# Soft-capped attention with a soft mixture of experts: ten instead of twelve output tiles stored by halves

## The chip, the core and the metric

The kernel runs on one core of a Trainium2 chip. The metric is the time of one execution on the device in microseconds (us). The core has five engines that run side by side and wait for each other by semaphores: PE multiplies matrices, DVE and ACT work element by element and are the ones that empty PE's accumulators (PSUM), POOL does the rest of the elementwise work and issues loads, and SP only issues transfers. The transfers themselves are carried by 16 DMA engines that all queues share.

## The reference

Two layers follow each other. The first is attention with a soft cap, for 8 batches, 12 heads, 448 tokens and 64 columns a head:

```
scores = cap * tanh(scale * q @ k.T / cap)
attn   = softmax(scores)
x      = (attn @ v), heads side by side: 3584 tokens x 768 columns
```

The second is a soft mixture of 8 experts with 4 slots each. Softmax over the tokens sends them into 32 slots, each expert runs two weight matrices over its slots, and softmax over the slots mixes the results back:

```
logits     = x @ phi                          # 3584 x 32
slot_input = softmax(logits, over tokens).T @ x
slot_out   = relu(slot_input @ w1[e]) @ w2[e] # 32 x 768
out        = softmax(logits, over slots) @ slot_out   # 3584 x 768, float32
```

What matters here is the last line: an output of 3584 x 768 floats, 11.01 MB, which must be written to DRAM, and which can be written only once slot_out is known.

## The kernel before, in words

**The long part.** The first 240 us or so are attention, with the logits and slot sums of the second layer woven in by a schedule written out by hand. Their order isn't touched by the change.

**The second layer's weights.** `layer1` (the first weight matrix, L1018) and `layer2` (the second, L1046) follow. The second matrix lies partly in SBUF (`w2b`) and partly in a DRAM copy that SP reads back (`w2t`, L997). `layer2` runs over 64 blocks twice, once for each half of the 768 output columns: the loop at L1099 makes `so[0]` (columns 0 to 383 of slot_out), the loop at L1106 makes `so[1]` (columns 384 to 767). `so[0]` is copied out of PSUM by ACT at L1104, `so[1]` by DVE at L1113.

**The output tiles.** The 3584 tokens are 28 tiles of 128 tokens. Tile n belongs to pair of batches `bb` = n // 7 and has place `c` = n % 7 in it; partition p of it holds token 896 bb + 7 p + c. So tiles that follow each other in one pair of batches hold neighbouring rows of the output, and two of them stored together are 6144 contiguous bytes a partition. Each tile is a matrix product of `et_tile` (the transposed exponentials) with `so`, then a multiplication by `winv` (one over the softmax sum) on the way from PSUM to SBUF, then a store by SP.

A tile goes out in one of two ways, and the constants `NH` and `NHL` (L1097) say which:

- Tiles 0 to NH - 1 go by halves, with `half_tile` (L1080). The first half (columns 0 to 383, called F here, so F10 is that of tile 10) needs only `so[0]`. F0 to F(NHL - 1) are made within the loop of `layer2` over the second half (L1109 to L1112), two a step on ACT and DVE and then one a step on ACT. F(NHL) to F(NH - 1) are made after it (L1114), with ACT for even tiles and DVE for odd ones; PE runs their products while DVE copies `so[1]`. Every F is a store of its own, 192 KB in rows of 1536 bytes. The second half (S) of the tiles below NH is made at L1130, with DVE for even tiles and ACT for odd ones. Two neighbouring S are stored together (384 KB, rows of 1536 bytes), unless the tile is the last of its pair of batches or the last below NH (L1092).
- Tiles from NH on go whole (W): two products into one PSUM tile (L1133), one multiplication over all 768 columns (ACT for even tiles at L1142, DVE for odd ones at L1140), and two neighbours stored together, 768 KB in rows of 6144 bytes (L1145). The seventh tile of a pair of batches is stored alone, as 384 KB.

**What else hangs on NH.** The transposition of the last two batches' exponentials (`e_transp`, L692 and L696) and their sums (`e_sums`, L705 and L706) stand in the same loop ahead of tiles NH + 3, NH + 5 and NH + 7. The PSUM tiles `op` of that loop come from a pool of three (L1128), so that the product of tile n waits until tile n - 3 has left PSUM. They take the place of the banks used before (`bank`, L1110 and L1115), so the first three of them wait for whoever read those banks last. The SBUF tiles `obh` (halves) and `ob` (whole) rotate through the eight places of tag `w1`; a place that held a stored tile is free when its store has landed.

**Order.** Each engine works through its instructions in the order of the program. SP issues the stores in the order F, S, W, and each store waits for the engines that wrote its source.

Of the kernel before, what the change touches and what calls it, by code (L numbers as in the profile page):

```python
# [37 lines left out]
def kernel(  # L38
# [1055 lines left out]
            return  # L1094
        store(k, half, half + 1, obs[bb, half][:, c - (n - k):c + 1, :], n - k + 1)

    NH, NHL = 12, 10  # L1097
    n2 = len(blocks)
    for n0 in range(0, n2, 4):  # L1099
        if n0 == n2 // 2 - 16:  # L1100
# [81 lines left out]
```

## Time and profile before

| what | value |
|---|---|
| median of 3 runs (lowest to highest) | 288.38 us (287.92 to 288.79) |
| the profiled execution, its own time | 288.24 us |
| its span, first to last instruction | 286.5 us |
| ACT, PE, DVE, POOL busy over the span | 89%, 87%, 85%, 48% |
| last product of PE ends | about 274 us |
| last store is issued | 276.0 us |
| stores of halves / of whole tiles | 19 / 9 |

The profiled execution is one of the program on the chip. Times within it are us from the first instruction. Shares of busy time are averages over the span; the part that the change touches is the last 31 us, from 255.6 us, when the first store is issued. GB/s are the bytes that the core's DMA engines moved in a stretch, and "DMA share" is how busy the 16 of them were (it can pass 1, since a DMA engine can have two packets under way).

### The profile page before, as it was taken

To read this page: it belongs to the slowest core of one execution; us is meant where nothing else is said; L and a number is where in the kernel's file an instruction comes from. 1 tells how busy PE (TensorE), PEld (TensorE's weight loads), DVE (VectorE), ACT (ScalarE), POOL (GpSimd) and SP (SyncE) were. 2 spreads that over 40 slices of the span, in tenths; PEclk is the share of its full clock that TensorE was granted. 3 is DMA by queue.
4 is the path that set the end of the run, shared out by engine and by line. 5 is a ranking of instruction groups with operands and counts; after the bars stand their busy time and mean duration, and the time that the engine had idled before them with its cause. 6 is when DMAs were issued, how large, how long until landed. Compare 5 with 4: busy or idle time off the path is not lost.

```text
span 286.5 us, 10763 instructions
## 1 busy us (share of the span) xinstructions
PE 250.3 (87%) x4706; PEld 170.3 (59%) x4706; DVE 242.6 (85%) x502; ACT 254.6 (89%) x211; POOL 138.9 (48%) x197
## 2 busy tenths in 40 slices
PE   8888889998999899989998999899899999998710
PEld 7555466756675666566656675667565767642400
DVE  3498999999999999999999999999999986437830
ACT  4999999999999999999999999999999997247720
POOL 7982655664765566555756646574563120200000
PEclk9999999999999999999999999999999999999975
DMA  7999999999999999999999999999999567989995
GB/s 241 257 205 205 201 194 204 224 205 206 232 230 196 209 232 225 217 206 231 227 216 198 226 224 211 214 226 222 206 182 226 137 247 223 409 326 392 414 420 244
DMA packets 58334, 68.11 MB, mean 238 GB/s; under 512 B 4144, under 2 KB 54448, under 8 KB 58288
## 3 DMA queue, kind: packets, MB, share of 16 engines
q0 software_dynamic: 42448, 35.31, 79.1%
q1 hardware_dynamic: 15552, 31.89, 31.7%
q8 instruction: 37, 0.61, 0.8%
q10 hardware_dynamic: 288, 0.23, 0.2%
q14 instruction: 9, 0.07, 0.1%
HBM read 91.72 MB, written 19.27 MB: 387 GB/s over the span
## 4 chain that ended last, share of the span: by engine, by line
DVE 40%; PE 33%; issue 10%; ACT 8%; POOL 5%; DMA 1%; DVEq 0%; ACTq 0%; SPq 0%
PE pv L590 9%; DVE xq L600 7%; PE sc L320 5%; DVE xp L570 4%; DVE xT L652 4%; DVE ex L571 4%; ACT ex L329 4%; DVE xp L568 3%; ACT ex L334 3%; DVE qT L279 3%; POOL vbd L287 2%; DVE ex L564 2%; DVE xp L569 2%; PE so_ps L1046 2%; DVE xf L566 2%
## 5 line engine op out<-in xcount | busy, mean ns | idle before, releaser
L329 ACT ACTIVATE ex<-sc 128x1344 f16<-128x1344 f32 (+1 forms) x113 | 148.3, 1428 | 1.4 <-PE sc L320 1.4
L334 ACT ACTIVATE ex<-ex 128x2688 bf16<-128x2688 f16 (+5 forms) x58 | 115.1, 1993 | 0.1
L590 PE MATMUL pv<-vbd,ex 128*128 128x130 bf16 (+1 forms) x1610 | 95.0, 211 | 11.4 <-POOL vbd L287 8.5
L590 PEld LDWEIGHTS <-ex 128*128 128x128 bf16 (+1 forms) x1680 | 75.7, 101 | 35.9 <-PE sc L320 9.0
L320 PE MATMUL sc<-qT,kT 64*64 64x448 bf16 x672 | 71.4, 360 | 0.5 <-DVE qT L279 0.4
L287 POOL CAST vbd<-vraw 64x896 bf16<-64x896 f32 x46 | 45.9, 998 | 49.5 <-issue 24.5
L600 DVE TENSOR_TENSOR xq<-pv,rec 128x448 bf16<-128x448 f32 x46 | 28.7, 625 | 1.6
L320 PEld LDWEIGHTS <-kT 64*64 64x64 bf16 x672 | 24.1, 105 | 6.3 <-issue 4.0
L295 POOL MEMSET vbd<- 64x1 bf16 x22 | 3.6, 165 | 45.7 <-PE pv L590 45.7
L570 DVE TENSOR_TENSOR xp<-xp,xf 128x1344 f16<-128x1344 f16 (+2 forms) x34 | 25.1, 738 | 0.8
L568 DVE TENSOR_TENSOR xp<-xp,xf 128x1344 f16<-128x1344 f16 (+2 forms) x34 | 25.0, 736 | 0.6
L116 POOL DMA_DIRECT2D w1b<-in_moe_w_dram x32 | 25.3, 792 | 0.0
L571 DVE TENSOR_TENSOR ex<-ex,xp 128x1344 uint16<-128x1344 uint16 (+2 forms) x34 | 24.7, 727 | 0.4
L567 DVE TENSOR_SCALAR xp<-xf 128x1344 f16<-128x1344 uint16 (+2 forms) x34 | 16.8, 494 | 0.4
L184 POOL DMA_DIRECT2D qb<-in_q_dram x22 | 16.7, 757 | 0.5 <-DMA kraw<-in_k_dram 0.5
L279 DVE COPY kT<-kps 128x896 bf16<-128x896 bf16 x23 | 14.2, 617 | 3.0 <-PE kps L274 2.8
L572 DVE TENSOR_SCALAR ex<-ex 128x1344 uint16<-128x1344 uint16 (+2 forms) x34 | 16.5, 485 | 0.1
L277 PEld LDWEIGHTS <-qb 128*64 128x64 bf16 x308 | 10.1, 109 | 10.9 <-issue 10.9
L184 POOL DMA_DIRECT2D kb<-in_k_dram x22 | 16.2, 735 | 0.1
L569 DVE TENSOR_SCALAR xp<-xp 128x1344 f16<-128x1344 f16 (+2 forms) x34 | 15.7, 462 | 0.6
L120 POOL DMA_DIRECT2D w2d<-in_moe_w_dram x21 | 15.9, 777 | 0.4 <-issue 0.4
L620 PE MATMUL pv<-ones 128*128 128x57 bf16 x376 | 16.0, 188 | 0.0
(124 smaller groups left out, 342.1 us busy)
## 6 DMA issues: line engine op xcount, KB each, us to landing
w1b<-in_moe_w_dram POOLq DMA_DIRECT2D x32, 384.0 KB, 9.1
vraw<-in_v_dram SPq DMA_DIRECT2D x44, 224.0 KB, 6.0
w2d<-in_moe_w_dram POOLq DMA_DIRECT2D x21, 384.0 KB, 8.1
w2t<-w2d SPq DMA_DIRECT2D x21, 384.0 KB, 7.1
out_dram<-ob SPq DMA_DIRECT2D x7, 768.0 KB, 8.2
qb<-in_q_dram POOLq DMA_DIRECT2D x22, 224.0 KB, 7.6
kb<-in_k_dram POOLq DMA_DIRECT2D x22, 224.0 KB, 6.1
w2b<-in_moe_w_dram POOLq DMA_DIRECT2D x11, 384.0 KB, 8.1
```

What stands on the lines that cost most here:

```text
L116: pool.dma_start(out=w1b[e][:, js, fs], in_=w1r[:, e, js, fs])
L184: pool.dma_start(out=t, in_=quad_ap(nm, Q))
L279: dve.tensor_copy(t, ps)
L287: pool.tensor_copy(vbds[Q % 2][r, :, :, c0:c0 + DH], raw[r])
L320: pe.matmul(sc[cs, u, 0:S], qkT["k", Q][r, c, cs], qkT["q", Q][r, :, cs], start=True, stop=True)
L329: act.activation(exs[j][:, half * CS + u0:half * CS + u1, :].bitcast(F16), (own[0] if i == u0 == 0 else sc)[:, u0:u1, 0:S], ACT.Tanh, scal ...
L334: act.activation(exs[j][:, u0:u1, :], exs[j][:, u0:u1, :].bitcast(F16), ACT.Exp, scale=cap)
L568: lambda: dve.tensor_tensor(p, p, f, op=ALU.mult),
L570: lambda: dve.tensor_tensor(p, p, f, op=ALU.mult),
L571: lambda: dve.tensor_tensor(y, y, p, op=ALU.add),
L590: pe.matmul(out_, exs[j][r, u, q0:q0 + (HP if tail else P)], v_, start=(c == 0 and g == gs[0] < NF), stop=(c == NT - 1), skip_group_check= ...
L600: dve.tensor_tensor(xq[Q][:, h, s0:s1, :], pv[:, 0:s1 - s0, 0:DH], rec.to_broadcast([P, s1 - s0, DH]), op=ALU.mult)
```

## The change

One constant goes from 12 to 10:

```diff
-    NH, NHL = 12, 10
+    NH, NHL = 10, 10
```

With it the loop at L1114 is empty, so F10 and F11 fall away, with their two products on PE, one multiplication each on ACT and DVE, and two stores. S0 to S9 are made as before, but S9 is now the last below NH and stored alone; S10 (which was stored with S9) and S11 (stored alone) fall away, again with one multiplication each on DVE and ACT. Tiles 10 and 11 become whole tiles: four products, one multiplication of 768 columns on ACT and one on DVE, and one store of 768 KB. The transpositions and sums of the last two batches now stand ahead of tiles 13, 15 and 17 instead of 15, 17 and 19. In counts: 28 stores become 26 (16 of halves, 10 of whole tiles); PE has the same products in another order; ACT and DVE have one instruction fewer each. The bytes written stay the same. POOL's instructions, and those of all engines ahead of L1113, are the same.

## The prediction

> **What bounds the kernel now.** I read the end of the execution first, since every edit lies there. The stretches of busy time:
>
> ```profile
> core 0: us, PE busy (x) PEld busy (x) DVE busy (x) ACT busy (x) POOL busy (x), PEclk, DMA share, GB/s
> ...
> 257.00:261.50 4.50, 4.06 (x42) 1.18 (x35) 3.00 (x6) 3.26 (x6) 0.00 (x0) 1.00 1.05 392
> ...
> 264.00:268.00 4.00, 3.46 (x23) 1.89 (x22) 3.40 (x6) 3.42 (x5) 0.00 (x0) 1.00 1.07 398
> 269.00:272.00 3.00, 1.98 (x11) 1.00 (x11) 2.46 (x3) 1.96 (x3) 0.00 (x0) 1.00 1.02 425
> 276.00:283.00 7.00, 0.00 (x0) 0.00 (x0) 0.00 (x0) 0.00 (x0) 0.00 (x0) 0.50 1.02 424
> ```
>
> The last two columns carry it. The DMA share is 1.02 to 1.07 from 257 us on, and after 276 us no engine computes: the transfers alone set the end, at 392 to 398 GB/s while rows of 1536 bytes go out (halves) and 424 or 425 with rows of 6144 (whole tiles). A DMA engine that never rests turns every pause in its supply into a later end. So the question isn't what ACT or DVE save but whether the stores still arrive without a gap. The transfers from 255 us on:
>
> ```profile
> issues: line engine op xcount, KB each, median us to landing
> out_dram<-ob SPq DMA_DIRECT2D x7, 768.0 KB, 8.2
> out_dram<-obh SPq DMA_DIRECT2D x14, 192.0 KB, 2.5
> out_dram<-obh SPq DMA_DIRECT2D x5, 384.0 KB, 3.7
> ```
>
> A small store lands 2.5 us after its issue, a whole pair 8.2 us: early stores hardly queue, late ones stand behind a long queue. So the early part is where a missing store can be felt. The chain of waits says what comes at the change:
>
> ```profile
> 259.68 0.57 DVE so L1113
> 260.25 0.04 issue
> 260.29 0.35 PE op L1086
> 260.64 0.03 issue
> 260.68 0.62 DVE obh L1088
> ```
>
> The S products need `so[1]`, whose copy ends at 260.25. F10 and F11 aren't on this chain. The timeline beside it:
>
> ```profile
> 259.22 1.29 ACT L1090 ACTIVATE obh<-op,winv 128x384 f32<-128x384 f32 x2
> ...
> 259.56 0.50 PE L1086 MATMUL op<-so,ET 128*128 128x384 bf16 x2
> 259.68 0.56 DVE L1113 CAST so<-so_ps 128x384 bf16<-128x384 f32 x1 [1.25 <-PE so_ps L1046]
> 260.15 2.38 DVE L1088 TENSOR_SCALAR obh<-op,winv 128x384 f32<-128x384 f32 x4
> ...
> 260.92 0.58 ACT L1090 ACTIVATE obh<-op,winv 128x384 f32<-128x384 f32 x1 [0.41 <-PE op L1086]
> ```
>
> The two products at 259.56 are F10 and F11; they run during the copy. ACT's group from 259.22 is F9 and F10, DVE's from 260.15 starts with F11, and 260.92 is S1 on ACT.
>
> **What is removed: supply.** Issue times on SP, from the trace: F0 255.64, then one F each 0.43 to 0.51 us up to F9 260.05, F10 260.56, F11 261.05; S0+S1 261.56, S2+S3 262.31, S4+S5 262.83, S6 263.34, S7+S8 264.03, S9+S10 264.94, S11 265.48, W12+W13 266.42.
>
> Each F is 196,608 bytes, 0.50 us at 392 GB/s; they come every 0.50 us, so supply and DMA go in step. In the trace's single packets (128 an F, counted in order) F0's first starts 0.84 us after its issue, with nothing ahead of it but 25 to 49 GB/s of leftover reading, and each from F2 to F11 1.00 us after. So only 0.16 us of work waits ahead of any F. F9's last packet starts at 261.56, F10's and F11's fill 261.56 to 262.58, and S0+S1 follows at 262.58. Without F10 and F11 the DMA engines have nothing after 261.56 until S0+S1 has been issued and has waited its 0.84 us.
>
> When is S0+S1 issued? Before, S1 leaves ACT at 261.50 and SP issues at 261.56, 0.06 later. S1's product started at 260.56, 0.05 after ACT had finished F10 (259.93 + 0.58 = 260.51): its PSUM bank was held by F10. In the new order of instructions that wait for ACT is gone, and S1's product can follow S0's (260.29) at PE's step between products of one tile, 0.16 us (264.36 to 264.52). So S1's product starts at 260.45, 0.11 earlier; ACT begins at 260.81 and ends at 261.39; SP issues at 261.45; first packet 261.45 + 0.84 = 262.29. **The gap is 262.29 - 261.56 = 0.73 us.**
>
> Bounds. If S1 isn't earlier and its first packet takes the loaded 1.02 us of the trace, the gap is 262.58 - 261.56 = 1.02. Below, S2+S3 holds the line: S3's product waits for S0 to leave PSUM (DVE, 261.29; its product starts at 261.34 already), and S0 depends on the copy of `so[1]`, which doesn't move. S2+S3 stays at 262.31 and can't flow before 263.15. Without a gap it would have started at 261.56 + 1.00 = 262.56, so at least 0.59 us is lost. I take 0.73, by the row of an unloaded store.
>
> **What is saved on the engines** is worth nothing. ACT loses two multiplications of 581 ns (F10 and S11) for one of 899, DVE two of 614 (F11, S10) for one of 1015: 0.26 and 0.21 us, and two issues of some 0.41 us go on SP. All of it is hidden by the transfers, which run on for 9 us after the last of them; with the cover gone it would be worth those 0.2 to 0.3 us.
>
> **What is saved on the DMA engines.** 786,432 bytes go as rows of 6144 instead of 1536: 1.98 us at 398 GB/s, 1.85 at 425. That is 0.13 us less. Its bounds are 0 (rates equal) and 0.16 (392 against 425).
>
> The Trainium skill speaks for the change here: DMA: Bandwidth & Descriptors, Rules for kernel authors, says to coalesce many small transfers into one large one. The trace agrees on the sign only; by that rule alone the sum would be the 0.13 us just worked out, without the gap.
>
> **What moves: the whole pair 10, 11.** With the gap at 0.73 the line of stores in flight becomes S0+S1 262.29, S2+S3 263.29, S4+S5 264.28, S6 265.26, S7+S8 265.76, S9 266.74, and the end of S9 at 267.23, by the packet times of before (each pair 0.98 to 1.00 us, a single 0.50). W10+W11 must be issued 0.84 us ahead of that, by 266.39. S9's multiplication starts on ACT at 263.72 as before; W10 follows it by the 0.53 us between ACT's starts, 264.25 to 265.15; W11's products wait for S8 to leave DVE (263.84) and its 1.02 us end at about 265.5. SP has S7+S8 until 264.84 and S9 until about 265.4, so W10+W11 goes out at about 265.5, 0.9 us in time. The transposition's copy (382 ns on DVE) now falls between W11 and W13, so W12+W13 is issued at about 266.8 instead of 266.42; it is needed by 267.23 + 1.85 - 0.84 = 268.2. From there the queue grows as before: 1.1 to 2.7 MB wait at each issue after 267.5. Reuse of `ob` places waits for landings of W10+W11 (about 270) and W12+W13 before tiles 21 and 23; a wait of 1 to 2 us there meets over 5 us of queue.
>
> **Sum.** 0.73 - 0.13 = +0.60 us on the profiled execution: 288.24 + 0.60 = 288.84. The median of the runs lies 0.14 above that execution, so the same sum from it gives 288.98. I say **288.9 us**. A measurement of this kernel tells about 0.3% (0.87 us) from no change; the forecast, +0.2%, lies within that.
>
> **Rivals.**
>
> *The gap closes.* F10 and F11 stop holding ACT, DVE and banks, and if S0+S1 and S2+S3 come so much earlier that no gap opens, the 0.13 us is all: 288.1 to 288.25. For it: S1 did wait for F10. Against it: the copy of `so[1]` at 259.68 to 260.25 holds S0, and through it S3; 0.59 us stays lost. In this case the rule of the Trainium skill on coalescing (DMA: Bandwidth & Descriptors, Rules for kernel authors) would have it right.
>
> *A second gap ahead of W10+W11: slower.* Nothing can be stored between S9 and the pair, which needs 0.90 us of ACT and 1.02 of DVE where halves needed 0.58. Each us past 266.39 is a us of idle transfer. It passes 0.87 us in all if the pair is issued after 266.39 + 0.27 = 266.7, 1.2 us later than I work out; at 267.2 the time is 289.7. For it: SP's issues already took 0.81 and 0.84 us at 264.03 and 265.48, and the products wait in a pool of three. Against it: two engines made the twelve S in 4.2 us, 2.36 MB at some 560 GB/s, faster than the DMA takes them, so the queue has 0.9 us in hand.
>
> *Faster: the gap hides an instruction fetch.* The tail of the trace has one DMA engine alone from 283.9 to 285.1, about 0.95 us behind the rest, as long as the single packet of 16 KB on the instruction queue at 272.64 (947 ns). If the new gap took that packet, 0.95 us would be won and the sum would be -0.35: 288.0. Together with a closed gap it would be over 1 us. Against it: the packet comes 10 us after the gap, and PE, whose 9412 instructions come to some 254 for each of the 37 such packets, has the same instructions from tile 12 on.
>
> **How the numbers follow.** The gap alone 0.72; the second gap 0.13; the closed gap 0.09; the fetch 0.06. Medians of three runs spread by 0.3 us to each side, so of the first case about a quarter would read as slower by over 0.3%: 0.72 x 0.24 + 0.13 = 0.30 slower. Faster by over 0.3% needs fetch and closed gap together, or luck: 0.05. The rest, 0.65, is within. The range: the forecast's bounds are 0.59 - 0.16 = +0.43 and 1.02 - 0 = +1.02, so 288.7 to 289.4 from the two bases; the closed gap takes it down to 288.2, and the near part of the second gap up to 289.6.
>
> **What would show it.** Right: 16 stores from `obh` and 10 from `ob`; a stretch at about 261.6 to 262.3 in which the DMA share falls to nearly nothing; S1's product at about 260.45; S0+S1 issued at about 261.45; all stores from then on landing late by the gap until tile 10, and the last packet 0.6 us later than 285.1. Wrong: a DMA share of 1 straight through 261 to 263 (the gap is closed), a second hole near 267 us, or a tail without the lone engine. An end that moves although transfers have no hole would say that the bound isn't the transfers at all.

## The result and the profile after

The changed kernel takes 289.39 us in the median of 7 runs (288.53 to 290.30), the kernel before 288.36 (287.92 to 289.05): a ratio of 1.0042, 95% interval 1.0027 to 1.0057. Run again (below) it came to 1.0019, interval 1.0004 to 1.0034. The change makes the kernel slower by 0.5 to 1.2 us.

The same stretches of the changed kernel, with the one added in which S0+S1 should arrive (columns as before, DMA share and GB/s last):

```profile
core 0: us, PE busy (x) PEld busy (x) DVE busy (x) ACT busy (x) POOL busy (x), PEclk, DMA share, GB/s
...
257.00:261.50 4.50, 3.45 (x41) 1.09 (x41) 2.52 (x5) 2.77 (x5) 0.00 (x0) 1.00 1.05 392
261.50:262.50 1.00, 0.82 (x4) 0.29 (x4) 0.95 (x2) 0.71 (x3) 0.00 (x0) 1.00 0.16 58
...
276.00:283.00 7.00, 0.00 (x0) 0.00 (x0) 1.38 (x2) 0.34 (x1) 0.00 (x0) 0.50 1.02 426
```

The same us of the kernel before:

```profile
261.50:262.50 1.00, 0.85 (x4) 0.29 (x3) 0.89 (x2) 0.81 (x3) 0.00 (x0) 1.00 1.06 387
```

The DMA share falls to 0.16 for one us, and from then on the engines are as full as before until the end. The changed kernel cut finer, and at the end of the transfers:

```profile
261.75:262.25 0.50, 0.46 (x3) 0.10 (x1) 0.45 (x2) 0.44 (x1) 0.00 (x0) 1.00 0.00 0
...
283.00:284.00 1.00, 0.00 (x0) 0.00 (x0) 0.00 (x0) 0.00 (x0) 0.00 (x0) 0.50 0.93 375
284.00:285.00 1.00, 0.00 (x0) 0.00 (x0) 0.00 (x0) 0.00 (x0) 0.00 (x0) 0.50 0.16 62
285.00:286.00 1.00, 0.00 (x0) 0.00 (x0) 0.00 (x0) 0.00 (x0) 0.00 (x0) 0.50 0.05 18
```

The end of the transfers in the kernel before:

```profile
283.00:284.00 1.00, 0.00 (x0) 0.00 (x0) 0.00 (x0) 0.00 (x0) 0.00 (x0) 0.50 0.40 160
284.00:285.00 1.00, 0.00 (x0) 0.00 (x0) 0.00 (x0) 0.00 (x0) 0.00 (x0) 0.50 0.06 25
285.00:286.00 1.00, 0.00 (x0) 0.00 (x0) 0.00 (x0) 0.00 (x0) 0.00 (x0) 0.50 0.00 0
```

Not a byte moves from 261.75 to 262.25. A share of 0.05 or 0.06 is one engine of 16: the lone engine is still there, in the last row of the changed kernel and in the last but one of the kernel before. The transfers of the changed kernel from 255 us on:

```profile
issues: line engine op xcount, KB each, median us to landing
out_dram<-ob SPq DMA_DIRECT2D x8, 768.0 KB, 7.9
out_dram<-obh SPq DMA_DIRECT2D x12, 192.0 KB, 2.0
out_dram<-obh SPq DMA_DIRECT2D x4, 384.0 KB, 2.7
```

And the timeline about the copy of `so[1]`:

```profile
259.78 0.56 DVE L1113 CAST so<-so_ps 128x384 bf16<-128x384 f32 x1 [1.25 <-PE so_ps L1046]
260.40 0.44 PEld L1086 LDWEIGHTS <-ET 128*128 128x128 bf16 x4 [1.05 <-DVE so L1113]
260.40 0.66 PE L1086 MATMUL op<-so,ET 128*128 128x384 bf16 x3 [0.67 <-DVE so L1113]
...
260.94 0.58 ACT L1090 ACTIVATE obh<-op,winv 128x384 f32<-128x384 f32 x1 [1.02 <-PE op L1086]
```

PE and ACT now stand idle about the copy (0.67 and 1.02 us), where the products of F10 and F11 ran and ACT worked on F10; S0 begins as soon as the copy is done, no sooner. This execution reached its first store 0.11 us later than the one before (255.75 against 255.64), so everything below is counted from the issue of F0.

### The profile page after: what moved, and what is told of

Same layout as the page of the kernel before. It is cut to its first block, busy times and chain, and to the rows that moved or that the text cites. A ratio compares the mean times of both kernels' runs of the same rounds, so it can differ in the third digit from the quotient of the medians.

```text
span 287.3 us, 10758 instructions
## 1 busy us (share of the span) xinstructions
PE 250.6 (87%) x4706; PEld 170.5 (59%) x4706; DVE 242.6 (84%) x501; ACT 254.2 (88%) x210; POOL 138.9 (48%) x197
## 4 chain that ended last, share of the span: by engine, by line
DVE 29%; PE 27%; ACT 26%; issue 9%; POOL 4%; DMA 2%; DVEq 0%; ACTq 0%
ACT ex L329 14%; ACT ex L334 10%; PE pv L590 6%; DVE xq L600 5%; PE sc L320 4%; DVE xp L570 3%; DVE ex L571 3%; DVE xT L652 3%; DMA out_dram<-ob 2%; PE so_ps L1046 2%; DVE xp L568 2%; PE hp L1018 2%; DVE qT L279 2%; POOL vbd L287 2%; DVE ex L564 2%
## 5 line engine op out<-in xcount | busy, mean ns | idle before, releaser
L571 DVE TENSOR_TENSOR ex<-ex,xp 128x1344 uint16<-128x1344 uint16 (+2 forms) x34 | 25.3, 744 | 0.4
L652 DVE COPY xT<-xps 128x896 bf16<-128x896 bf16 (+1 forms) x24 | 14.3, 597 | 1.7 <-PE xps L643 1.7
```

The costliest lines, as they stand in the source:

```text
L571: lambda: dve.tensor_tensor(y, y, p, op=ALU.add),
L652: copy(xTs[Q][:, hs[0]:hs[-1] + 1, :], ps[:, hs[0]:hs[-1] + 1, :])
```

## The experiments

The theory is the forecast's: the DMA engines set the end, and they rest while S0+S1 isn't there. Its rivals: the other things that the change moves (transpositions, whole pair) cost the time, or it isn't lost in the transfers. One table for all runs; a ratio is to the kernel before, run beside it on the same chip. "Pause" is the time that the DMA engines went without a packet, as a mean of the 16, from 0.9 us behind F0's issue until half of them had finished for good; "half done" is that point, "last packet" the end of the last one. "Behind" is from the last landing to the end of the span, all these from one profiled execution. "Outside" is the time less the span, a mean over all runs of the kernel.

| kernel | ratio (95% interval) | pause | half done | last packet | behind | outside |
|---|---|---|---|---|---|---|
| before | | 0.08 | 27.74 | 29.46 | 1.02 | 1.79 |
| e9, before again | 1.0007 (0.9994 to 1.0020) | 0.07 | 27.74 | 29.44 | 1.02 | 1.79 |
| after | 1.0042 (1.0027 to 1.0057) | 0.90 | 28.42 | 30.02 | 1.14 | 2.04 |
| e1, after again | 1.0019 (1.0004 to 1.0034) | 0.90 | 28.42 | 30.13 | 1.15 | 2.01 |
| e2, gap fed | 1.0025 (1.0010 to 1.0040) | 0.08 | 28.60 | 30.35 | 1.02 | 1.81 |
| e3, fed late | 1.0036 (1.0021 to 1.0050) | 0.89 | 29.40 | 31.16 | 1.02 | 1.83 |
| e4, eight | 1.0034 (1.0018 to 1.0049) | 1.15 | 28.58 | 30.40 | 1.27 | 1.78 |
| e5, fourteen | 1.0020 (1.0007 to 1.0033) | 0.07 | 27.86 | 29.62 | 1.32 | 1.78 |
| e6, old places | 1.0031 (1.0017 to 1.0045) | 0.92 | 28.42 | 30.14 | 1.15 | 2.00 |
| e7, split | 1.0009 (0.9995 to 1.0022) | 0.10 | 27.76 | 29.49 | 1.03 | 1.84 |
| e10, before, fewer products | 1.0015 (0.9998 to 1.0031) | 0.98 | 28.70 | 29.51 | 1.03 | 1.77 |
| e11, after, fewer products | 1.0005 (0.9992 to 1.0018) | 1.27 | 28.88 | 29.73 | 1.14 | 2.03 |
| e12, after, SP padded | 1.0024 (1.0010 to 1.0037) | 0.89 | 28.42 | 30.00 | 0.90 | 1.82 |
| e13, after, more products | 1.0013 (0.9992 to 1.0034) | 1.91 | 29.58 | 29.94 | 1.15 | 1.98 |

The times of one kernel scatter by about 0.5 us from run to run (standard deviation), so the ratios tell little finer than 0.4 us. Within the trace, the half-done point of the same program repeats to 0.02 us (two executions of the kernel before, two of the changed one), and that is what the verdicts rest on.

**Both kernels again (e1, e9).** Nothing edited.

> The changed kernel once more. Gap theory (the DMA engines rest for 0.77 us between S9's forerunner F9 and S0+S1, which comes back at the end, less some 0.13 to 0.2 us for longer rows): +0.6 us against the kernel before, in the trace a stretch without packets of 0.7 to 0.8 us near 261.7. Rival (the two executions differ ahead of the stores, and the change itself does nothing): a difference that falls to 0 with more rounds. The first comparison gave a ratio of 1.0042 (1.0027 to 1.0057), +1.2 us, twice what the gap gives; if that is the size, something beside the gap costs 0.6 us.

> The kernel before against itself: both theories 0. It tells how far two medians of the same program lie apart, against which +0.6 and +1.2 us have to be read: a difference of up to 0.3 us either way is expected.

The kernel before against itself differs by 0.2 us, with 0 inside the interval. The changed one is 0.68 us later at the half-done point, three times the same (with e6), and its pause is 0.83 us longer. The difference of the two, 0.15 us, is what is left for the longer rows.

**Feed the gap (e2), or the same bytes later (e3).** Two extra tiles of 192 KB, written to a scratch place:

```diff
+    for n in range(2):
+        sp.dma_start(out=dram.tile([P, HD], F32, name=f"extra{n}"), in_=obs[1, 0][:, 1 + n, :])
     dve.tensor_copy(so[1], so_ps[1])
```

That is e2, F8 and F9 once more; e3 stands behind the store of tiles 12 and 13:

```diff
+        if n == NH + 3:
+            for m in range(2):
+                sp.dma_start(out=dram.tile([P, HD], F32, name=f"extra{m}"), in_=ob[:, 0, m, :])
```

> The changed kernel, which also writes two tiles of 192 KB (F8 and F9 once more, 1.00 us of transfers) to a scratch place in DRAM, issued right behind F9, where the gap is. Gap theory: 0.77 us of the 1.00 is free, and S0+S1 starts some 0.3 us later: 0.2 to 0.3 us over the changed kernel. Rival (the transfers have no real pause there, and the time is lost elsewhere): 1.0 us over it.

> The same two extra tiles of 192 KB, issued behind the store of tiles 12 and 13, where the queue is long. Both theories: all of their 1.0 us shows, 1.0 us over the changed kernel. It is the measure for the run that feeds the gap: by the gap theory this one is 0.7 us slower than that one, by the rival they are equal.

The stretches of e2 in which the gap was; this execution issued F0 at 254.80, 0.95 us ahead of the changed kernel's, so the gap would lie at about 260.8 to 261.5:

```profile
260.00:261.00 1.00, 0.60 (x3) 0.19 (x2) 0.97 (x2) 0.71 (x2) 0.00 (x0) 1.00 1.06 393
261.00:262.00 1.00, 0.83 (x3) 0.29 (x3) 0.77 (x2) 0.97 (x2) 0.00 (x0) 1.00 1.04 381
```

The gap is full, and the half-done point is 0.18 us later than that of the changed kernel (28.60 against 28.42); the same bytes sent later cost 0.98 (29.40). So 0.80 us of transfer time was free where the gap lies, and none behind tiles 12 and 13. These two runs show that the DMA engines rest there and that it is time they don't get back. In time e3 lies 0.44 us above e2 (medians 289.45 and 289.01): the same way, but hardly more than the ratios can tell.

**A larger and a smaller number of halves (e4, e5).** `NH, NHL = 8, 8` and `NH, NHL = 14, 10`.

> Eight tiles by halves instead of ten: two fewer F again, and PE reaches the copy of so[1] about 0.5 us sooner, as F8 and F9 no longer stand between its products. Gap theory: the gap grows by 1.00 - 0.5 us to about 1.25 us and another 0.13 us is saved by longer rows: 0.3 to 0.4 us over the changed kernel, about 1.0 over the one before. Rival (the place of the moved transpositions, or the whole pair, is what costs): transpositions and first whole pair move by two tiles again, so a step as large as the first one, 0.6 to 1.2 us over the changed kernel, whatever the gap.

> Fourteen tiles by halves, with F10 to F13 made behind the copy of so[1]. Gap theory: the kernel before has no gap to close, so more supply brings nothing, and four more rows of 1536 bytes a partition cost 0.13 us: 0 to +0.2 us against the kernel before, no pause in the transfers. Rival (halves are simply better than whole tiles at this place): another 0.6 us faster than the kernel before.

In e4 the gap lies a little earlier and is wider:

```profile
260.00:261.00 1.00, 0.81 (x3) 0.29 (x3) 0.95 (x3) 0.71 (x2) 0.00 (x0) 1.00 0.09 32
```

Two more tiles taken from the halves cost only 0.16 us more to the half-done point (the pause is 0.25 longer, so that 0.09 is left for the longer rows), some 0.33 to the last packet: not a second step of 0.68, as the rival wanted, because `so[1]` comes sooner too (S0+S1 is issued 5.03 us behind F0, against 5.79). Fourteen halves have no pause and cost 0.12 us, which is the price of the shorter rows measured without a gap beside it. Its ratio, +0.6 us, is more than the expected 0 to 0.2 and than the transfers explain. 0.30 us of it lies behind the last landing (1.32 against 1.02); 0.34 us there pass between two closing instructions of SP that stand 0.06 apart in before, after, e2, e4 and e12. Why is open.

**The transpositions at their old places (e6).** `NH + 3`, `+ 5`, `+ 7` become `NH + 5`, `+ 7`, `+ 9`.

> The changed kernel with the transpositions and sums of the last two batches ahead of tiles 15, 17 and 19, as before the change. Gap theory: the gap stays, the time is that of the changed kernel within 0.1 us, so +0.6 us against the kernel before. Rival (their earlier place delays the first whole tiles): the time of the kernel before, 0.

Pause, half-done point and last packet are those of the changed kernel. Where the transpositions stand makes no difference that these numbers show.

**An earlier first store (e7).** The copy of `so[0]` in two parts:

```diff
-    act.copy(so[0], so_ps[0])
+    act.copy(so[0][:, 0:160], so_ps[0][:, 0:160])
+    dve.tensor_copy(so[0][:, 160:HD], so_ps[0][:, 160:HD])
```

> The kernel before (twelve tiles by halves) with the copy of so[0] split, 160 columns on ACT and 224 on DVE, so that F0 and with it the first packet comes about 0.15 us sooner; so[1] stays. Gap theory: the transfers set the end from the first packet on, so an earlier start is won as long as S0+S1 keeps up (it has 0.18 us to spare, 262.58 against 261.56 + 0.84): 0.1 to 0.15 us faster in the trace, from first packet of F0 to the end the same. Rival (PE or the copy of so[1] sets the end): no change.

The edit didn't do what it was meant to:

```profile
254.10 0.29 ACT L1104 CAST so<-so_ps 128x160 bf16<-128x160 f32 x1 [2.89 <-PE so_ps L1046]
254.43 0.39 DVE L1105 CAST so<-so_ps 128x224 bf16<-128x224 f32 x1 [2.27 <-ACT so L1104]
```

DVE's part waited for ACT's ("<-ACT so"), so F0 was issued 1.74 us behind the start of the copy instead of 1.51. From F0's issue to the half-done point the time stayed, as the theory has it; the earlier start wasn't tested.

**The lone engine and PE's instructions (e10, e11, e13).** One packet of 16 KB on the instruction queue, 0.95 us long, is the suspect for the lone engine's delay. The edits change only the number of products that keep PE busy and whose results are never read. In e10 (the kernel before) and e11 (the changed one) 70 PE instructions are left out:

```diff
-    FILL = (... (7, 'a', fill, 24), ...)
+    FILL = (... (7, 'a', fill, 19), ...)
```

In e13 (the changed kernel) there are 86 more:

```diff
-    FILL = (... (7, 'a', fill, 24), ...)
+    FILL = (... (7, 'a', fill, 30), ...)
...
-    busy(27)
+    busy(28)
```

> The kernel before with 35 fewer of the products that only keep PE busy (fill at the step after 7: 19 instead of 24, in seven batches; their results are never read), 70 fewer PE instructions. Theory: the DMA engine that ends alone is late because the last 16 KB of PE's instructions are fetched through it while stores wait; the fetches come at the same places of PE's instructions in every run (before about the 9420th of 9441), so with 70 fewer this last one is never asked for, and the last packet comes 0.9 to 1.1 us sooner against the first store's issue: 1 us faster. Rival (that engine is slow by itself, or takes more of the bytes): the tail of 1.3 to 1.7 us with one engine stays, no change.

> The changed kernel with the same 35 products left out. If the lone engine's tail and the gap are two separate costs, the tail's 0.9 to 1.1 us go here too, and the difference to the kernel before with the same edit stays that of the change: 0.65 us within the transfers, 0.6 to 0.9 us in all. Rival (the lone engine makes up for the gap or the gap for it): a difference under 0.3 us or over 1.2.

> The changed kernel with 43 more of the products that only keep PE busy (fill at the step after 7: 30 instead of 24 in seven batches, and one at the start), 86 more PE instructions. It is the third rival of the prediction made on purpose: the last fetch of PE's instructions hangs on how far PE has come, and with 86 more ahead it should be asked for where PE waits for so[1], and run between 260.8 and 262.0 us, in or just ahead of the gap, instead of at 270 in the full queue. If the gap can hide it, the lone engine's tail (1.3 to 1.5 us between the other engines' end and the last packet) shrinks by 0.6 to 0.9 us and the last packet comes 29.2 to 29.5 us behind the first store's issue instead of 30.0 to 30.1: 0.6 us faster than the changed kernel, about the time of the kernel before. If not (the fetch holds SP's issue up, as it did where 35 products were left out), the gap grows by as much as the tail shrinks, and the last packet stays at 30.0 or later.

Half of the expectation of e10 held: the 37th packet is gone, and the lone engine's tail (last packet less half done) fell from 1.72 to 0.81 us. But it fell because the other engines were done 0.96 us later; the last packet came no sooner. For the 36th, which had run at 254.6, ahead of the stores, now ran from 257.34 to 258.70 in their midst, and the stretches of e10 show what happened then:

```profile
257.00:258.00 1.00, 1.00 (x15) 0.31 (x18) 0.68 (x2) 0.71 (x2) 0.00 (x0) 1.00 1.10 391
258.00:259.00 1.00, 1.00 (x18) 0.24 (x10) 0.55 (x1) 0.71 (x2) 0.00 (x0) 1.00 0.63 229
259.00:260.00 1.00, 1.00 (x15) 0.30 (x11) 0.20 (x1) 0.80 (x2) 0.00 (x0) 1.00 0.45 167
```

During the fetch all engines still had packets. From about 258.7, when it ended, to 259.6 only about one packet at a time was under way, so some 15 of the 16 engines rested. SP's issues suggest why. The stores by halves in e10 by their line in the code, with the shortest, median and longest issue in ns and the first and last start:

```profile
L1074 SPq DMA_DIRECT2D out_dram<-obh x19: 337/410/1411, 255.8 to 266.6; - x19
```

The same row of e13:

```profile
L1074 SPq DMA_DIRECT2D out_dram<-obh x16: 338/415/2382, 255.4 to 265.7; - x16
```

In e10 the issue at 257.67 took 1411 ns, in e11 the one at 257.32 1713 ns, in e13 the one at 258.91 2382 ns, where one usually takes 410. In all three it ended 0.37 or 0.38 us behind the end of the fetch. So I read it thus: SP didn't hand out the next store while one engine was held up, and the fetch became a pause for all. It was 0.98 us in e10, the last packet came as late as before (29.51 against 29.46), and the expected 1 us was not won. In e13 the fetch came at 258.9 and lasted 2.02 us, not between 260.8 and 262.0 as aimed; the pause grew by 1.0 us as the tail shrank to 0.36, near the second case of the expectation (last packet 29.94, against 30.02 and 30.13 in the changed kernel). In e11 the pause of the fetch came early enough (258.3 to 259.6) for S0+S1 to catch up, and the gap at 261 was gone: 1.27 us of pause, not 0.98 + 0.83. The expected 0.6 to 0.9 us against e10 shrank to 0.2 in the transfers, and the medians of the two are equal within 0.1 us (288.47 and 288.51), as the rival had it. Two pauses in one line of stores don't add up when the second is a wait for a fixed moment.

The Trainium skill (Runtime: NRT & Kernel Launch, Instruction fetch mechanics) puts the cost of crossing a 16 KiB block at one update of a DMA tail, mostly hidden. It has the size right, 16,384 bytes a packet here; what it cost differs where it fell among this kernel's stores: about 1 us of pause in e10, e11 and e13. What the fetches in the attention part cost, no run here shows.

**What lies behind the transfers (e12).** Four loads of 2 KB into a scratch place, issued by SP in the attention part of the changed kernel:

```diff
+    def small(n):
+        for m in range(n):
+            sp.dma_start(out=dram.tile([16, NS], F32, name=f"small{m}"), in_=moe_phi[0:16, :])
+
+    at(20, "b", small, 4)
```

> The changed kernel with four loads of 2 KB into a scratch place by SP in the middle of the attention part, so that SP has again as many instructions as in the kernel before. Theory: of the change's cost some 0.35 us isn't in the transfers but in how SP's instructions end (one fetch of 8 KB that comes 1.8 us behind the span's end instead of 1.0, and five waits instead of three behind the landing of the last store): with four more, the time outside the span falls from 2.02 to 1.78 us, and one wait instead of five is left behind the last landing, 0.25 us less in the span. 0.5 us faster than the changed kernel, the gap of 0.75 us and its 0.68 us in the transfers as they were. Rival (the time outside the span goes with the gap or the later end): outside stays at 2.0 us.

The gap stayed (0.89, half done at 28.42), "outside" fell from 2.0 to 1.82 us and "behind" from 1.15 to 0.90. The 0.5 us expected in time isn't shown: in the mean e12 lies 0.66 us above the kernel before, ten halves without the loads 0.88, a difference within the scatter. Behind the last landing SP goes through landing semaphores in a fixed order, 0.06 us each: three are left before, five after, seven in e4, one in e5 and e12. Two DMAs fewer on SP leave two more, two DMAs more leave two fewer. Outside, one fetch of 8 KB on another instruction queue moves. The DMA row of the kernel before from 286.5 to 290 us, in 40 slices of 0.09 us:

```profile
DMA  0000000000300000000000000000000000000000
```

The same row of the changed kernel:

```profile
DMA  0000000000000000000000000000040000000000
```

It starts at 287.4 us before, 0.96 behind the end of the span, and at 289.1 after, 1.80 behind. In e12 it is 1.19 behind. Over all runs the time outside is 1.77 to 1.84 us where the profiled fetch starts at most 1.55 us behind the end of the span, or where the trace has none behind it (e4, e5), and 1.98 to 2.04 where it starts 1.79 us or more behind (after, e1, e6, e11, e13). The two go together; that one causes the other isn't shown.

No version here beats the kernel before.

## Why the prediction was right, and where it was off

The forecast was +0.60 us; the two comparisons give +1.2 (0.8 to 1.6) and +0.55 (0.1 to 1.0). Point by point:

- **The bound.** Right: e3's bytes cost their full 0.98 us in a full queue, and e2's only 0.18 in the gap.
- **The gap.** Forecast 0.73 us, between bounds of 0.59 and 1.02. F9's last packet started at 261.68 and S0+S1's first at 262.45: 0.77. S1's product did come 0.09 us sooner behind the copy of `so[1]` (forecast 0.11), S0+S1 was issued at 261.54, 261.43 by the clock of the execution before (forecast 261.45), and its first packet came 0.91 us later (forecast 0.84). S2+S3 was issued at 262.41, 262.30 by that clock (forecast 262.31).
- **The saving by longer rows.** Forecast 0.13 us; the pause of 0.83 less the 0.68 at the half-done point leaves 0.15, and e5, which has no pause, measures 0.12 for the next two tiles.
- **The whole pair.** Forecast at 265.5 and the next at 266.8; issued at 265.61 and 266.91, less the 0.11 of a later start exactly these. No second gap: in the trace the transfers run on without one.
- **The sum in the transfers.** Forecast 0.60; last packet 0.57, 0.68 and 0.69 later in three profiles.
- **The term that was mis-sized: what lies behind the transfers.** The prediction took the stretch behind the last landing and the time outside the span as they were, and costed SP's two fewer issues at nothing. They cost 0.12 us (1.02 to 1.14, other order of the last waits) and 0.23 us (1.79 to 2.02). Over the 30 runs of ten halves in the three comparisons (with e6) the span grew by 0.65 us in the mean and the time by 0.88, about the forecast and this term together (0.95). That the first comparison's 289.39 lay inside the range is partly luck: it is at the top of the bounds for the gap alone (289.4), and a third of the distance came from a term that isn't in the sum. Of the chances, the larger one (0.65, within 0.3%) has the second comparison's ratio of 1.0019 on its side, the smaller one (0.30, slower by more) the first comparison's 1.0042.
- **The rivals.** The closed gap and the second gap are out by the trace. The fetch that hides in the gap didn't happen in the changed kernel (its last fetch ran at 270.35), and e13, which was made for it, missed the gap by 2 us. What the runs do show speaks against it: a fetch among the stores made idle time in e10, e11 and e13, and only a pause ahead of the gap (e11) overlapped with it.

What stays open: what ties the 0.2 us outside the span to the fetch of 8 KB, where the 0.30 us behind the last landing of e5 comes from, why PE's fetch in e13 came 2 us sooner than aimed, and what a fetch in the gap itself would cost.

## What to carry to other kernels

When the transfers set the end and supply goes in step with them, an output piece that is made while something else is being waited for is worth the idle transfer time that it fills (here 0.83 us of pause against 1.00 us of transfers), even if making it costs an engine more than the alternative: look at what the DMA engines do at the moment from which pieces are taken, not at the count of instructions or stores. To prove such a gap, feed it: the same bytes cost little there and their full time elsewhere. And an edit that changes a count of instructions can move the fetches and the order of the last waits with it, here some 0.1 to 0.4 us behind the last landing and outside the span that have nothing to do with what the edit does.

## What the hardware showed that was not expected

The three fetches of 16 KB of instructions that fell among stores issued one by one took 1355 ns (e10), 1738 (e11) and 2021 (e13); the late one in the full queue took 947 in the kernel before. The store that SP issued meanwhile took 1411, 1713 and 2382 ns instead of 410, each ending 0.37 or 0.38 us behind the fetch, and some 15 of the 16 engines then had no packet for about 1 us.

With the fetch late in the full queue nothing paused, and one engine ended 1.6 to 1.8 us behind the half-done point, in every run that has it there; in e10 and e11, which have no such fetch, it was 0.8, in e13 0.4. That the lone engine is the one that carried the fetch is inferred from this: the trace doesn't say on which engine a packet ran. In none of these three did the last packet come sooner than in the kernel before.
